# Block 0's rows of heads 2 to 7 by casting DMA issues ahead of the constants, and one ring of three PSUM tiles for its turns and scores

## The chip, the cores and the metric

One NeuronCore of one Trainium2 chip runs the kernel. The metric is the device time of one execution in microseconds. Before the change it is 240.57 us, the median of 7 runs (240.35 to 241.47).

## The reference, cut to what matters

Chunked attention with a small memory goes straight into a gated feed-forward layer:

```python
q, k, v: (4, 8, 768, 64)    mem_k, mem_v: (4, 8, 8, 64)      # batch, heads, tokens, width
for each chunk of 32 tokens:
    k_full = [mem_k, k[start-16 : start+32+8]]               # 8 memory rows, then the neighbourhood
    a = softmax(q_chunk @ k_full.T / 8);  out_chunk = a @ v_full
x = out as (3072 tokens, 512)
y = (relu(x @ w_gate) * (x @ w_val)) @ w_out                 # 512 -> 1536 -> 512, float32 out
```

## The kernel before, in words

The 3072 tokens are worked in 8 blocks of 384 (`TB`); two blocks make one batch entry. A block is cut into 4 pieces of 96 queries (`NQ`, `QB`), and the key window of each piece has 128 rows: 8 of memory and 120 of the sequence. Heads go in 4 pairs, called `hp`. All matmuls are in 16 bits.

Three kinds of work make a block. **Attention** turns keys and queries so that the head width lies on partitions, multiplies them to scores, takes the exponential on ScalarE, sums it and multiplies it with the values. **The first layer** is 12 units (`ffn_unit`, 4 gate and 4 value matmuls of 128x384 each, then a Relu on ScalarE at L340 and a product on VectorE at L341). **The second layer** is 3 output units (`out_unit`, 12 matmuls of 128x512 and a copy). While TensorE runs the layers of block n, the attention of block n+1 is woven between the units.

The order on every engine is written by hand (`tc.manual_schedule()`, L69): each engine does its instructions in the order of the source, and waits where data or a buffer is missing. The change touches the first three blocks:

- **Start.** `kst` and `qst` (L80, L81) hold float32 rows of block 0's keys and queries for heads 0 to 3. They come in two parts each by the hardware queues of SyncE and ScalarE (L384 to L388) and are cast by `cast` (L445) on VectorE and ScalarE. Heads 4 to 7 come by issues of GpSimd that cast on the way (`load_rows`, L125, L436, L438). GpSimd first makes the constants `ident` and `sel` (L431 to L434), then fetches the whole `mem_v` into `memv` (L435), then these rows, then block 0's value windows (`load_band`, L130, called at L439), `memk`, and the first weights (`load_w`, 256 columns of both matrices at a time, L442 and L443). SyncE copies the memory rows of `memv` into the value windows by `load_mem_v` (L149).
- **Block 0's attention** (L461 to L509). `fill` (L379) keeps TensorE running until the rows are there. `turn_pe` (L177) turns keys and queries of one pair by matmuls against `sel` and `ident` into a PSUM tile, `turn_copy` (L196) brings it to SBUF. `step_s0` (L236) makes mask and scores, and the exponential `ex` (L245). `wide_d` (L272) sums `ex` by matmuls into `xs` and takes the logarithm in place (L278); `wide_e` (L280) makes the reciprocal `rw` of it by an exponential (L282). `wide_v` (L285) multiplies with the values into `xo` and scales into `xT` (L291). The PSUM tiles of the kernel fill 8 banks of 128x512 float32: `xo` and `xs` take one each, the tile `sc` of the pool `sps` two, and the other four are first two turn tiles (`tps`), later the four banks of the units (`fps`).
- **Unit chunks.** The first two units are opened together, and each `chunk(0, f)` (L456) needs only pair f of `xT`, so that they start as soon as the first pair is done.
- **Block 1** (L524 to L558). Its turns, scores (`step_s`, L248), sums and products stand between units 2 to 11 of block 0.
- **Block 2** (L614, L615, in `run`, L585). While the units of block 1 run, `run` places pair hp's turn after the unit `at[hp] - 1`, its scores after the unit `at[hp]`, and its products inside the unit `at[hp] + 2`. From block 3 on, keys and queries are turned by DMA.

Of the kernel before, what the change touches and what calls it, by code (L numbers as in the profile page):

```python
# [17 lines left out]
def kernel(  # L18
# [12 lines left out]
    nc = tc.nc  # L31
# [33 lines left out]

    sps = ctx.enter_context(tc.tile_pool(name="sps", bufs=1, space=bass.MemoryType.PSUM))
    xps = ctx.enter_context(tc.tile_pool(name="xps", bufs=1, space=bass.MemoryType.PSUM))
# [11 lines left out]
    sels = [const.tile([128, NQ, 32], F16, name=f"sel{p}") for p in range(2)]  # L79
    kst = const.tile([KR + 2, H // 2, J * D], F32, name="kst")  # L80
    qst = const.tile([QR, H // 2, J * D], F32, name="qst")  # L81
    k16s = [const.tile([128, NQ, H, D], F16, name=f"k16{p}") for p in range(2)]

    vwins = [const.tile([128, NQ, H, 2 * D], F16, name=f"vwin{p}") for p in range(2)]
    qbds = [const.tile([128, NQ, HP, 2, QB], F16, name=f"qbd{p}") for p in range(2)]
    memk, memv = (const.tile([NMEM, B * H, D], F16, name=nm) for nm in ("memk", "memv"))
    ones = const.tile([128, 3, D], F16, name="ones")
    bias = const.tile([128, 3], F32, name="bias")
# [31 lines left out]
    def load_rows_mem(dma, dst, n, h0, nh):  # L120
        src = bass.AP(tensor=mem_k.tensor, offset=mem_k[n // 2, h0, 0, 0].offset,
                      ap=[[J * D, 2], [NMEM * D, nh], [1, J * D]])
        dma(dst, src)

    def load_rows(n, h0, nh):  # L125
        rk, rq = rows_of(n)
        pool_dma(rk[0:KR, h0:h0 + nh], k_rows(n, h0, nh))
        pool_dma(rq[:, h0:h0 + nh], q_rows(n, h0, nh))

# [47 lines left out]
    def turn_pe(n, hp):  # L177

        if n != 1:
            pool, tag = (pools["t"], "t") if n == 0 else (sps, "sc")  # L180
            ps = pool.tile([128, 2, 512], F32, tag=tag, name="kq_ps")
            kps, qps = ps[:, 0], ps[:, 1, 0:TB]
        else:
            ps, kps, qps = None, bank("k_ps"), bank("q_ps")[:, 0:TB]
        turns[n, hp] = ps, kps, qps
        rk, rq = (t.rearrange("p h (j d) -> p h j d", j=J) for t in rows_of(n))
        sel = sels[n % 2].rearrange("p i t -> p (i t)")

        for t, dst, w in ((rk, kps, sel[0:KR + 2]), (rq, qps, ident[:QR, :QR])):
            steps = dst.rearrange("p (r j) -> p j r", j=J) if n == 0 else dst.rearrange("p (j r) -> p j r", j=J)  # L190
            for j in range(J):
                for hh in range(2):
                    nc.tensor.matmul(steps[D * hh:D * hh + D, j], lhsT=t[:, 2 * hp + hh, j], rhs=w,
                                     start=True, stop=True)

    def turn_copy(n, hp):  # L196
# [5 lines left out]
        ps, kps, qps = turns.pop((n, hp))  # L202
        if n == 0:
            dve_copy(turns[n][:, hp], ps.rearrange("p a c -> p (a c)")[:, 0:512 + TB])
# [31 lines left out]
    def step_s0(n, hp):  # L236

        sc = sps.tile([128, 2, 512], F32, tag="sc", name="sc_ps")
        mq = bass.AP(tensor=maskq.tensor, offset=maskq.offset, ap=[maskq.ap[0], [0, NQ], [1, QB]])
# [8 lines left out]
    def step_s(n, hp):  # L248
        sc = sps.tile([128, 2, 512], F32, tag="sc", name="sc_ps")
        view = sc[:, :, 0:TB].rearrange("p a (c m) -> p a c m", m=QB)  # L250
# [21 lines left out]
    def wide_d(n, hp):  # L272
        ex = exs[n, hp]
        for i0, i1, kind in ((0, 1, 1), (1, NQ, 0)) if n == 0 else ((0, NQ - 1, 0), (NQ - 1, NQ, 2)):
            for hh in range(2):
                nc.tensor.matmul(xs[D * hh:D * hh + D, QB * i0:QB * i1], lhsT=ones[:, kind, :],
                                 rhs=ex[:, hh, i0:i1, :], start=True, stop=True)
        nc.scalar.activation(xs, xs, ACT.Ln, scale=1.0 / 64.0)  # L278

    def wide_e(n, hp):  # L280
        rinv = rpool.tile([128, TB], F32, tag="rw", bufs=4, name="rw")
        nc.scalar.activation(rinv, xs, ACT.Exp, scale=-1.0, bias=mln64)  # L282
        rinvs[n, hp] = rinv

    def wide_v(n, hp):  # L285
        ex = exs.pop((n, hp))
        for i in range(NQ):
            for hh in range(2):
                nc.tensor.matmul(xo[D * hh:D * hh + D, QB * i:QB * i + QB], lhsT=vwins[n][:, i, 2 * hp + hh, 0:D],  # L289
                                 rhs=ex[:, hh, i, :], start=True, stop=True)  # L290
        nc.vector.tensor_tensor(out=x_of(n)[:, hp, :], in0=xo, in1=rinvs.pop((n, hp)), op=ALU.mult)  # L291

# [27 lines left out]
    def ffn_open(n, ms, spare=False):  # L320
# [3 lines left out]
        for m in ms:  # L324
            if spare:
                sc = sps.tile([128, 2, 512], F32, tag="sc", name="gv_ps")
                pair = sc[:, 0, 0:TB], sc[:, 1, 0:TB]
# [55 lines left out]

    for hp in range(HP // 2):  # L384
        sp(kst[0:KR, 2 * hp:2 * hp + 2], k_rows(0, 2 * hp, 2))
        act_dma(qst[:, 2 * hp:2 * hp + 2], q_rows(0, 2 * hp, 2))
        if hp == 0:
            load_rows_mem(sp, kst[KR:KR + 2], 0, 0, H // 2)  # L388
    nc.scalar.preload_act_table_set("natural_log_exp_and_others")

    def words(t):
        return t.bitcast(U32)

    zero(words(filler), 0)


# [33 lines left out]

    nc.gpsimd.memset(words(ident), 0)  # L431
    nc.gpsimd.memset(words(sels[0].rearrange("p i t -> p (i t)")), 0)
    select(ident, 1.0, 0, [[-1, 128]], 1)
    build_sel(0)  # L434
    fetch_mem(memv, mem_v)  # L435
    load_rows(0, 4, 2)  # L436
    load_rows_mem(pool_dma, rows_of(0)[0][KR:KR + 2, H // 2:H], 0, H // 2, H // 2)
    load_rows(0, 6, 2)  # L438
    load_band(0, v, vwins)  # L439
    load_mem_v(0)  # L440
    fetch_mem(memk, mem_k)
    load_w(0, 256)  # L442
    load_w(256, 512)  # L443

    def cast(t, hp, eng):  # L445
        dst, src, n = rows_of(0)[t], (kst, qst)[t], (KR + 2, QR)[t]
        eng(dst[0:n, 2 * hp:2 * hp + 2], src[:, 2 * hp:2 * hp + 2])

# [11 lines left out]

    with tc.tile_pool(name="tps", bufs=2, space=bass.MemoryType.PSUM) as pools["t"]:  # L461
        fill(12)
        cast(0, 0, dve_copy)
        for t, hp in ((1, 0), (1, 1), (0, 1)):
            cast(t, hp, act_copy)
        turn_pe(0, 0)
        turn_copy(0, 0)
        fill(4)
        step_s0(0, 0)
        turn_pe(0, 1)  # L470
        turn_copy(0, 1)
        wide_d(0, 0)
        wide_e(0, 0)
        step_s0(0, 1)
        turn_pe(0, 2)
        turn_copy(0, 2)
        wide_d(0, 1)
        wide_e(0, 1)
        turn_pe(0, 3)
        turn_copy(0, 3)  # L480
    pools["f"] = ctx.enter_context(tc.tile_pool(name="fps", bufs=4, space=bass.MemoryType.PSUM))
    step_s0(0, 2)
    wide_v(0, 0)
    wide_d(0, 2)
    step_s0(0, 3)
    wide_e(0, 2)


    build_sel(1)
    load_rows_mem(pool_dma, rows_of(1)[0][KR:KR + 2], 1, 0, H)  # L490
    load_rows(1, 0, 4)
    load_rows(1, 4, 4)

    select(bias, NEG, -NMEM, [[-32, 3]], 1, ALU.is_ge)
    select(bias, 0.0, -NMEM, [[0, 3]], 1, ALU.is_ge)
    select(bias, NEG, NMEM + 55, [[32, 3]], -1, ALU.is_ge)
    load_w(512, 768)
    load_w(768, 1024)

    ffn_open(0, (0, 1))  # L500
    wide_v(0, 1)
    wide_d(0, 3)
    wide_e(0, 3)
    chunk(0, 0)
    wide_v(0, 2)
    chunk(0, 1)
# [3 lines left out]
    ffn_close(0)  # L510
    zero(vwins[1][96:128, NQ - 1, :, 0:D], 0.0)
    load_band(1, v, vwins)
    load_mem_v(1)
    load_w(1024, 1280)
    load_w(1280, 1536)
    load_rows_mem(pool_dma, rows_of(2)[0][KR:KR + 2], 2, 0, H)
    load_rows(2, 0, 4)
    load_rows(2, 4, 4)

    def sums(n, hp):  # L520
        wide_d(n, hp)
        wide_e(n, hp)

    ffn_unit(0, 2, spare=True)  # L524
    ffn_unit(0, 3)
    turn_pe(1, 0)
    turn_copy(1, 0)
    turn_pe(1, 1)
    turn_copy(1, 1)
    step_s(1, 0)  # L530
    turn_pe(1, 2)
    turn_copy(1, 2)
    ffn_unit(0, 4)
    step_s(1, 1)
    sums(1, 0)
    ffn_unit(0, 5)
    turn_pe(1, 3)
    turn_copy(1, 3)
    step_s(1, 2)
    sums(1, 1)  # L540
    ffn_unit(0, 6)
    step_s(1, 3)
    ffn_unit(0, 7)
    wide_v(1, 0)
    sums(1, 2)
    ffn_unit(0, 8)
    wide_v(1, 1)
    sums(1, 3)
    one_words(0, 0, 128, 0, 1, ONE)
    ffn_unit(0, 9)  # L550
    wide_v(1, 2)
    one_words(0, 0, NMEM + 16, 0, 1, 0)
    one_words(0, 0, NMEM, 0, 1, ONE)
    ffn_unit(0, 10)
    wide_v(1, 3)
    one_words(0, 0, 128, 1, 2, ONE)
# [5 lines left out]
    for a in range(0, NDC, 4):  # L562
        pool_dma(wo[:, a:a + 4, :], wo_src[:, a:a + 4, :])
    zero(words(k16s[0][0:32, 0].rearrange("p h d -> p (h d)")), 0)
    zero(words(k16s[1][96:128, NQ - 1].rearrange("p h d -> p (h d)")), 0)

# [18 lines left out]
    def run(order, n, at, turn_at):  # L585
        for u, (b, x) in enumerate(order):
# [3 lines left out]
            inner, outer = ("ve", "") if x >= NDC else ("v", "e")  # L590
            unit(b, x, [lambda w=(w, hp): pieces(n, [w]) for hp in now for w in inner])
            pieces(n, [(w, hp) for hp in now for w in outer])
            if n < NB:
                pieces(n, [("s", hp) for hp in range(HP) if u == at[hp]])
            if n == 2:
                for hp in range(HP):
                    if u == at[hp] - 1:
                        turn_pe(n, hp)
                        turn_copy(n, hp)
                if u < len(clear):  # L600
                    clear[u]()
            if u == turn_at and n + 1 < NB:
# [46 lines left out]
```

## Time and profile before

| What | Value |
|---|---|
| median of 7 runs | 240.57 us |
| the profiled execution, its own time | 241.84 us |
| its span, first to last instruction | 239.9 us |
| mean granted TensorE clock | 0.986 |
| TensorE / ScalarE / GpSimd / VectorE busy | 229.6 / 142.3 / 101.5 / 105.5 us |
| DMA, mean over the span | 115 GB/s, 107831 packets |
| unit 2 of block 0 starts on TensorE | 23.48 us |
| first turn of block 1 | 26.17 us |
| unit 0 of block 1 | 43.60 us |
| first output unit | 66.53 us |

The profile is one execution taken by the hardware profiler, on its one core. A line of the time order gives start and length in microseconds, the engine, the source line, the operation, what it writes and reads, how many, and in brackets the idle time before it with what ended that. Matmuls overlap, so their lengths are longer than the distance of their starts. In a table of stretches each engine has its busy time and its instruction count, then come the granted TensorE clock (1.00 is full), the busy share of the DMA engines and GB/s. In the table of waits a line names the engine and line that waited, for whom, and the total, the number and the longest.

### The profile page before, as it was taken

To read this page: it belongs to the slowest core of one execution; us is meant where nothing else is said; L and a number is where in the kernel's file an instruction comes from. 1 tells how busy PE (TensorE), PEld (TensorE's weight loads), DVE (VectorE), ACT (ScalarE), POOL (GpSimd) and SP (SyncE) were. 2 spreads that over 40 slices of the span, in tenths; PEclk is the share of its full clock that TensorE was granted. 3 is DMA by queue.
4 is the path that set the end of the run, shared out by engine and by line. 5 is a ranking of instruction groups with operands and counts; after the bars stand their busy time and mean duration, and the time that the engine had idled before them with its cause. 6 is when DMAs were issued, how large, how long until landed. Compare 5 with 4: busy or idle time off the path is not lost.

```text
span 239.9 us, 4610 instructions
## 1 busy us (share of the span) xinstructions
PE 229.6 (96%) x1736; PEld 132.4 (55%) x1736; DVE 105.5 (44%) x208; ACT 142.3 (59%) x300; POOL 101.5 (42%) x129
## 2 busy tenths in 40 slices
PE   7969899999899999999999999999999999999993
PEld 4634555655544566646664566546664666556641
DVE  3442846878621046521663055604642166313400
ACT  3671497277644288926984579728892698434321
POOL 8997766857039800794069501990220000000000
PEclk9985999999999999999999999999999999999999
DMA  7999999999987999299929998699901100120012
GB/s 163 135 163 193 194 179 194 179 198 151 149 117 91 198 128 154 44 146 170 155 54 98 162 190 75 42 190 152 137 3 60 71 3 0 43 91 0 1 44 87
DMA packets 107831, 27.61 MB, mean 115 GB/s; under 512 B 91730, under 2 KB 104866, under 8 KB 107810
## 3 DMA queue, kind: packets, MB, share of 16 engines
q0 software_dynamic: 82560, 15.16, 78.8%
q1 hardware_dynamic: 21378, 5.61, 20.4%
q10 hardware_dynamic: 3872, 6.56, 8.3%
q8 instruction: 13, 0.21, 0.4%
q14 instruction: 8, 0.07, 0.1%
HBM read 31.13 MB, written 6.29 MB: 156 GB/s over the span
## 4 chain that ended last, share of the span: by engine, by line
PE 81%; DVE 5%; POOL 4%; DMA 4%; ACT 3%; issue 2%; POOLq 0%; DVEq 0%
PE o_ps L360 25%; PE g_ps L334 24%; PE v_ps L334 23%; DMA wv<-in_moe_w_val_dram 3%; PE sc_ps L258 3%; DVE kq L207 3%; DVE gv L341 2%; PE xo_ps L298 2%; PE xs_ps L298 2%; POOL vwin L136 2%; PE sc_ps L233 1%; PE xo_ps L289 1%; ACT gr L340 1%; DMA out_dram<-o_sb 1%; ACT ln L302 1%
## 5 line engine op out<-in xcount | busy, mean ns | idle before, releaser
L341 DVE TENSOR_TENSOR gv<-v_ps,gr 128x384 f16<-128x384 f32 x95 | 52.8, 557 | 98.0 <-ACT gr L340 86.7
L334 PE MATMUL v_ps<-xT,wv 128*128 128x384 f16 x380 | 79.5, 329 | 0.4 <-DMA wv<-in_moe_w_val_dram 0.4
L334 PE MATMUL g_ps<-xT,wg 128*128 128x384 f16 x380 | 79.7, 330 | 0.0
L360 PE MATMUL o_ps<-wo,gv 128*128 128x512 f16 x288 | 63.5, 379 | 0.0
L340 ACT ACTIVATE gr<-g_ps 128x384 f16<-128x384 f32 x95 | 46.1, 487 | 21.9 <-PE g_ps L334 11.9
L334 PEld LDWEIGHTS <-wv 128*128 128x128 f16 x384 | 36.6, 99 | 22.9 <-DMA wv<-in_moe_w_val_dram 0.8
L334 PEld LDWEIGHTS <-wg 128*128 128x128 f16 x384 | 36.3, 98 | 23.0 <-issue 1.0
L360 PEld LDWEIGHTS <-gv 128*128 128x128 f16 x288 | 28.1, 98 | 32.9
L221 POOL COPY qbd<-qT 64x1536 f16<-64x1536 f16 x10 | 14.6, 1462 | 59.6 <-DMA qT<-q16n 59.3
L264 ACT ACTIVATE ex<-sc_ps,bias 128x256 f16<-128x256 f32 x84 | 33.4, 468 | 7.2 <-PE sc_ps L233 6.5
L369 ACT COPY o_sb<-o_ps 128x512 f32<-128x512 f32 x23 | 13.5, 586 | 39.2 <-PE o_ps L360 33.2
L136 POOL DMA_DIRECT2D vwin<-in_v_dram x32 | 29.0, 924 | 3.4 <-PE v_ps L334 1.0
L307 ACT ACTIVATE rinv<-ln,mln 64x768 f32<-64x768 f32 x24 | 22.1, 923 | 0.0
L302 ACT ACTIVATE ln<-xo_ps 64x384 f32<-64x384 f32 x24 | 11.7, 487 | 14.7 <-PE xs_ps L298 14.7
L136 POOL DMA_DIRECT2D k<-in_k_dram x20 | 17.8, 900 | 0.6 <-issue 0.6
L313 DVE TENSOR_TENSOR xT<-xo_ps,rinv 64x384 f16<-64x384 f32 x24 | 13.1, 547 | 10.2 <-ACT rinv L307 10.2
L162 POOL DMA_DIRECT2D q16n<-in_q_dram x20 | 15.5, 796 | 4.2 <-DMA wo<-in_moe_w_out_dram 4.2
L313 DVE TENSOR_TENSOR xT<-xs_ps,rinv 64x384 f16<-64x384 f32 x24 | 13.2, 551 | 0.7
L298 PEld LDWEIGHTS <-vwin 128*128 128x128 f16 x192 | 10.8, 98 | 3.2
L302 ACT ACTIVATE ln<-xs_ps 64x384 f32<-64x384 f32 x24 | 11.4, 474 | 0.0
L298 PE MATMUL xo_ps<-ex,vwin 128*128 128x96 f16 x96 | 11.1, 206 | 0.0
L298 PE MATMUL xs_ps<-ex,vwin 128*128 128x96 f16 x96 | 11.1, 206 | 0.0
(73 smaller groups left out, 134.1 us busy)
## 6 DMA issues: line engine op xcount, KB each, us to landing
out_dram<-o_sb ACTq DMA_DIRECT2D x23, 256.0 KB
vwin<-in_v_dram POOLq DMA_DIRECT2D x24, 120.0 KB, 8.6
q16n<-in_q_dram POOLq DMA_DIRECT2D x20, 96.0 KB, 5.6
k<-in_k_dram POOLq DMA_DIRECT2D x15, 120.0 KB, 4.4
wg<-in_moe_w_gate_dram POOLq DMA_DIRECT2D x6, 256.0 KB, 7.8
wv<-in_moe_w_val_dram POOLq DMA_DIRECT2D x6, 256.0 KB, 8.1
wo<-in_moe_w_out_dram POOLq DMA_DIRECT2D x3, 512.0 KB, 9.9
rk<-in_k_dram POOLq DMA_DIRECT2D x4, 224.0 KB, 8.6
```

The costliest lines, as they stand in the source:

```text
L136: pool_dma(dsts[p][NMEM + m0:NMEM + m1, i, :, 0:D], src)
L162: pool_dma(q16s[n][:, i], src)
L221: nc.gpsimd.tensor_copy(qbds[n % 2][s, :, :, hh, :].rearrange("p i a m -> p (i a) m"), qTs[n][s].rearrange("p i a m -> p (i a) m"))
L264: nc.scalar.activation(flat[:, :, :, s], view[:, :, :, s], ACT.Exp, scale=SCALE, bias=bias[:, g:g + 1])
L298: nc.tensor.matmul((xo, xs)[hh][:, QB * i:QB * i + QB], lhsT=vw[:, i, 2 * hp + hh, :], rhs=ex[:, hh, i, :], start=True, stop=True)
L302: nc.scalar.activation(ln[:, hh], (xo, xs)[hh][D:128], ACT.Ln, scale=1.0 / 64.0)
L307: nc.scalar.activation(rinv, lns.pop((n, hp)), ACT.Exp, scale=-1.0, bias=mln64[0:D, :])
L313: nc.vector.tensor_tensor(out=x_of(n)[D * hh:D * hh + D, hp, :], in0=(xo, xs)[hh][0:D], in1=rinv[:, hh, :], op=ALU.mult)
L334: nc.tensor.matmul(ps[a], lhsT=(wg, wv)[a][:, f, 128 * m:128 * m + 128], rhs=xTs[n][:, f, :], start=(f == 0), stop=(f == NFC - 1))
L340: nc.scalar.activation(gr, g_ps, ACT.Relu)
L341: nc.vector.tensor_tensor(out=gvs[n][:, m, :], in0=v_ps, in1=gr, op=ALU.mult)
L360: nc.tensor.matmul(o_ps, lhsT=gvs[n][:, m, 128 * t:128 * t + 128], rhs=wo[:, m, :], start=(m == 0), stop=(m == NDC - 1))
```

## The change

Only heads 0 and 1 of block 0 come by the hardware queues, as one issue for keys and one for queries; SyncE also brings the memory values of batch entry 0 as float32 (`mem32`), cast to `mem16` on VectorE. VectorE copies `mem16` into the 4 value windows of block 0, GpSimd into those of block 1, so that `memv` and `memk` are fetched later. GpSimd issues the rows of heads 2 and 3 and the keys of heads 4 to 7 before it makes `ident` and `sel`, whose clearing goes to VectorE, and the queries of heads 4 to 7 after them. In block 0 the turns and scores take turns in one ring of three tiles of two banks each; their order changes, `sps` opens only after that ring is closed, 10 fills stand in place of 12 and 4. The logarithm of `wide_d` goes to `rw` instead of staying in `xs`, and `wide_e` is joined to it. In block 1 all four turns and two scores stand before unit 4, the products of all four pairs stand between units 9 and 10, and they alternate between `xo` and `xs`. In block 2 the turn of a pair stands inside the unit `at[hp] - 1`, between its gate and value matmuls. The third weight part is issued ahead of the selects for `bias`, block 1's values after the fifth.

```diff
-    kst = const.tile([KR + 2, H // 2, J * D], F32, name="kst")
-    qst = const.tile([QR, H // 2, J * D], F32, name="qst")
+    kst = const.tile([KR + 2, 2, J * D], F32, name="kst")
+    qst = const.tile([QR, 2, J * D], F32, name="qst")
...
-            pool, tag = (pools["t"], "t") if n == 0 else (sps, "sc")
+            pool, tag = (pools["t"], "t") if n == 0 else (pools["s"], "sc")
...
-        if n == 0:
+        if n == 0 and hp == 0:
+            dve_copy(turns[n][:, hp, 0:512], kps)
+            act_copy(turns[n][:, hp, 512:], qps)
+        elif n == 0:
             dve_copy(turns[n][:, hp], ps.rearrange("p a c -> p (a c)")[:, 0:512 + TB])
...
     def step_s0(n, hp):
-        sc = sps.tile([128, 2, 512], F32, tag="sc", name="sc_ps")
+        sc = pools["t"].tile([128, 2, 512], F32, tag="t", name="sc_ps")
...
-        nc.scalar.activation(xs, xs, ACT.Ln, scale=1.0 / 64.0)
-
-    def wide_e(n, hp):
         rinv = rpool.tile([128, TB], F32, tag="rw", bufs=4, name="rw")
-        nc.scalar.activation(rinv, xs, ACT.Exp, scale=-1.0, bias=mln64)
+        nc.scalar.activation(rinv, xs, ACT.Ln, scale=1.0 / 64.0)
+        nc.scalar.activation(rinv, rinv, ACT.Exp, scale=-1.0, bias=mln64)
...
     def wide_v(n, hp):
+        xo_ = xs if n == 1 and hp % 2 else xo
...
-    for hp in range(HP // 2):
-        sp(kst[0:KR, 2 * hp:2 * hp + 2], k_rows(0, 2 * hp, 2))
-        act_dma(qst[:, 2 * hp:2 * hp + 2], q_rows(0, 2 * hp, 2))
-        if hp == 0:
-            load_rows_mem(sp, kst[KR:KR + 2], 0, 0, H // 2)
+    sp(kst[0:KR], k_rows(0, 0, 2))
+    act_dma(qst, q_rows(0, 0, 2))
+    load_rows_mem(sp, kst[KR:KR + 2], 0, 0, 2)
+    sp(mem32, bass.AP(tensor=mem_v.tensor, offset=mem_v[0, 0, 0, 0].offset,
+                      ap=[[D, NMEM], [NMEM * D, H], [1, D]]))
...
-    nc.gpsimd.memset(words(ident), 0)
-    nc.gpsimd.memset(words(sels[0].rearrange("p i t -> p (i t)")), 0)
+    load_k(0, 2, 2)
+    load_rows_mem(pool_dma, rows_of(0)[0][KR:KR + 2, 2:H], 0, 2, H - 2)
+    load_q(0, 2, 2)
+    load_k(0, 4, 4)
     select(ident, 1.0, 0, [[-1, 128]], 1)
     build_sel(0)
-    fetch_mem(memv, mem_v)
-    load_rows(0, 4, 2)
-    load_rows_mem(pool_dma, rows_of(0)[0][KR:KR + 2, H // 2:H], 0, H // 2, H // 2)
-    load_rows(0, 6, 2)
+    load_q(0, 4, 4)
     load_band(0, v, vwins)
-    load_mem_v(0)
-    fetch_mem(memk, mem_k)
     load_w(0, 256)
     load_w(256, 512)
...
+    with tc.tile_pool(name="tps", bufs=3, space=bass.MemoryType.PSUM) as pools["t"]:
+        fill(10)
+        dve_copy(rows_of(0)[0][0:KR + 2, 0:2], kst)
+        act_copy(rows_of(0)[1][:, 0:2], qst)
+        dve_copy(mem16, mem32)
+        mem_values = [lambda i=i: dve_copy(vwins[0][0:NMEM, i, :, 0:D], mem16) for i in range(NQ)]
+        mem_values[0]()
         turn_pe(0, 0)
         turn_copy(0, 0)
-        fill(4)
-        step_s0(0, 0)
         turn_pe(0, 1)
         turn_copy(0, 1)
-        wide_d(0, 0)
-        wide_e(0, 0)
-        step_s0(0, 1)
+        step_s0(0, 0)
+        for i in range(1, NQ):
+            mem_values[i]()
         turn_pe(0, 2)
         turn_copy(0, 2)
-        wide_d(0, 1)
-        wide_e(0, 1)
+        step_s0(0, 1)
+        wide_d(0, 0)
         turn_pe(0, 3)
         turn_copy(0, 3)
+        step_s0(0, 2)
+        wide_d(0, 1)
+        step_s0(0, 3)
     pools["f"] = ctx.enter_context(tc.tile_pool(name="fps", bufs=4, space=bass.MemoryType.PSUM))
-    step_s0(0, 2)
+    pools["s"] = ctx.enter_context(tc.tile_pool(name="sps", bufs=1, space=bass.MemoryType.PSUM))
     wide_v(0, 0)
     wide_d(0, 2)
-    step_s0(0, 3)
-    wide_e(0, 2)
+    wide_v(0, 1)
...
     ffn_open(0, (0, 1))
-    wide_v(0, 1)
+    wide_v(0, 2)
     wide_d(0, 3)
-    wide_e(0, 3)
     chunk(0, 0)
-    wide_v(0, 2)
     chunk(0, 1)
     wide_v(0, 3)
...
-    turn_pe(1, 0)
-    turn_copy(1, 0)
-    turn_pe(1, 1)
-    turn_copy(1, 1)
+    for hp in range(2):
+        turn_pe(1, hp)
+        turn_copy(1, hp)
     step_s(1, 0)
-    turn_pe(1, 2)
-    turn_copy(1, 2)
+    for hp in range(2, HP):
+        turn_pe(1, hp)
+        turn_copy(1, hp)
+    step_s(1, 1)
+    wide_d(1, 0)
     ffn_unit(0, 4)
-    step_s(1, 1)
-    sums(1, 0)
+    step_s(1, 2)
+    wide_d(1, 1)
     ffn_unit(0, 5)
-    turn_pe(1, 3)
-    turn_copy(1, 3)
-    step_s(1, 2)
-    sums(1, 1)
+    step_s(1, 3)
+    wide_d(1, 2)
     ffn_unit(0, 6)
-    step_s(1, 3)
+    wide_d(1, 3)
     ffn_unit(0, 7)
-    wide_v(1, 0)
-    sums(1, 2)
+    one_words(0, 0, 128, 0, 1, ONE)
     ffn_unit(0, 8)
-    wide_v(1, 1)
-    sums(1, 3)
-    one_words(0, 0, 128, 0, 1, ONE)
     ffn_unit(0, 9)
-    wide_v(1, 2)
+    for hp in range(HP):
+        wide_v(1, hp)
...
-            unit(b, x, [lambda w=(w, hp): pieces(n, [w]) for hp in now for w in inner])
+            turning = [hp for hp in range(HP) if n == 2 and u == at[hp] - 1]
+            unit(b, x, [lambda hp=hp: (turn_pe(n, hp), turn_copy(n, hp)) for hp in turning]
+                 + [lambda w=(w, hp): pieces(n, [w]) for hp in now for w in inner])
```

## The prediction

> **What bounds the kernel now.** I read the page's slices first (TensorE full after about 24 us), then the table of stretches, the order of time around 12 to 24 us, the chain that ended last, and the waits. From the 66.53 us mark TensorE never stops, so a microsecond won before it is kept. The page:
>
> ```profile
> PE 229.6 (96%) x1736; PEld 132.4 (55%) x1736; DVE 105.5 (44%) x208; ACT 142.3 (59%) x300; POOL 101.5 (42%) x129
> PEclk9985999999999999999999999999999999999999
> ```
>
> The clock line has one hole, at 12 to 24 us. The table of stretches places it:
>
> ```profile
> 12.00:13.00 1.00, 1.00 (x20) 0.54 (x17) 0.95 (x2) 0.83 (x2) 1.00 (x2) 1.00 1.73 125
> 15.00:16.00 1.00, 0.47 (x16) 0.30 (x11) 0.41 (x1) 0.77 (x2) 1.00 (x3) 1.00 1.41 180
> 16.00:17.00 1.00, 0.44 (x4) 0.18 (x3) 0.14 (x1) 0.51 (x2) 0.62 (x2) 0.61 1.47 191
> 17.00:18.00 1.00, 0.56 (x4) 0.14 (x3) 0.00 (x0) 0.84 (x2) 0.93 (x3) 0.50 1.52 199
> 22.00:23.00 1.00, 1.00 (x5) 0.49 (x4) 0.10 (x1) 0.00 (x0) 1.00 (x2) 0.50 1.44 194
> 23.00:24.00 1.00, 1.00 (x8) 0.60 (x7) 0.30 (x1) 0.83 (x2) 1.00 (x2) 0.98 1.45 196
> ```
>
> TensorE (first column) is half idle from 15 us, the clock halves inside the slice at 16 (0.61 = 22% full, so at 16.22) and is back at 23.04. Two idle stretches stand around it in the order of time:
>
> ```profile
> 16.56 0.53 PE L276 MATMUL xs_ps<-ex,ones 128*64 128x96 f16 x4 [1.08 <-ACT rw L282]
> 17.96 0.50 PE L334 MATMUL v_ps<-xT,wv 128*128 128x384 f16 x1 [0.44 <-DMA wv<-in_moe_w_val_dram]
> ```
>
> The first is `xs` waiting for the exponential that still reads it. The second is the first value weights. The chain says why they are late: GpSimd's issue queue from the start, then one long flight:
>
> ```profile
> 1.85 0.83 POOL memv L139
> ...
> 9.55 0.67 POOL memk L139
> ...
> 10.95 6.97 DMA wv<-in_moe_w_val_dram
> ```
>
> The waits hold the third thing, the scores of blocks 1 and 2 behind the copies of their turns:
>
> ```profile
> PE sc_ps L233 <- DVE kq L207: 2.9, 6, 0.7
> ```
>
> Four of the six are block 2's, 0.50 or 0.51 each in the order of time.
>
> **The queue and the start.** GpSimd loses `memv` (0.85 us) and `memk` (0.72) ahead of the weights, two clears (0.15 each), and keeps as many row issues (0.6 to 0.76 each; those of four heads took 0.72 to 0.76). Its first issue starts at 0.81 instead of 1.83, its value weights at 0.81 + 0.70 + 0.60 + 0.65 + 0.73 + 0.76 (selects, 0.29 + 0.47) + 0.67 + 3.7 (values) + 0.84 = 9.5 instead of 10.95. The flight shortens too: SyncE's small copies out of `memv` go until later, and by the packet records the 512-byte packets ran at 240 to 340 per us at 13 to 16 us beside these copies, and at 380 after them. Values (3,700 packets of 128 bytes at about 950 per us) start when the rows are done, about 7.3, and land by about 11.8 (before 13.3); gate and value weights follow at 1.33 us each, 13.2 and 14.5 (before 16.6 and 17.92). Needed below: 13.4 and 16.1. Three us of slack cover an error here.
>
> First, heads 0 and 1 by hardware. The first key part landed at 4.67, with the second queued behind it, so its loss speeds nothing: cast at 4.7, turn at 5.2 as before. Rows on the casting queue took 3.6 to 4.8 us from issue to landing: heads 2 and 3 land at about 5.8, after 448-packet issues the last keys at 7.3, the last queries (issued 4.25) at 8.4. Their turns come at 6.5 and 8.35: no stall, or 0.5 if the first packets wait until 4.87 as in this trace. `ident` and `sel` are ready at 4.25, 0.9 us ahead.
>
> In the program as built, the ScalarE half of pair 0's copy waits for VectorE's half: 0.68 + 0.5 us in a row for one copy of 1.09. The turn of pair 1 (1.0 us) covers it. The copies of `mem16` stand in no row; between a small clear (0.09) and the 114x512 cast (0.43), I take 0.25, near the cast. They stand on VectorE ahead of pair 2's copy and delay it by 0.75 (0.3 to 1.3), under scores of pair 1; beyond 1.5 TensorE would wait. GpSimd's four copies cost below 0.5 each (a third of the 64x1536 copy's 1.46), and delay only weights needed 10 us later.
>
> TensorE's list then adds up from its rows (turn 1.0, the first 1.3; mask and scores 0.85; sum and product 0.35 each): turn 0 until 6.5, turn 1 7.5, scores 0 8.35, turn 2 9.3, scores 1 10.15, sum 0 10.5, turn 3 11.45, scores 2 12.3, sum 1 12.65, scores 3 13.4, product 0 13.75. On ScalarE ex takes 0.81, Ln 0.47, Exp 0.58: ex 3 until 14.9, Ln 2 15.3, Exp 2 15.9, Exp 3 17.1. `xs` is now free after the Ln, so the 1.08 wait goes. Late next is `xo`: product, 0.12, scaling 0.55, again. Products 1 and 2 start at 14.5 and 15.5, sum 3 ends at 16.1, and chunk 0 runs from there. Chunks 1 and 2, product 3 and its scaling (until 18.5) and chunk 3 give unit 2 at **19.2 at full clock, against 23.48**: −4.3.
>
> **The clock.** Between 12.81 and 16.22 TensorE idles 1.15 us by this list. The slices of before give 2.2 busy us in those 3.4, mine 2.3: nearly the same. [...] But before, the longest gap was 1.08 us, and it dropped. I take the row: it drops at 16.2 again. [...] The sixteen matmuls, 0.16 each at full clock, cost 0.32 until 19.63; unit 2 at 20.8: **−2.7**.
>
> [...]
>
> **Block 1.** Scores are drawn ahead and turn 3 stands before unit 4, so ScalarE's work is packed into units 4 to 7. Starts of ScalarE in the order of time:
>
> ```profile
> 32.71 0.48 ACT L340 ACTIVATE gr<-g_ps 128x384 f16<-128x384 f32 x1
> 33.09 1.21 ACT L264 ACTIVATE ex<-sc_ps,bias 128x256 f16<-128x256 f32 x3
> 34.18 0.50 ACT L278 ACTIVATE xs_ps<-xs_ps 128x384 f32<-128x384 f32 x1
> 34.71 0.58 ACT L282 ACTIVATE rw<-xs_ps,mln 128x384 f32<-128x384 f32 x1
> 35.19 0.48 ACT L340 ACTIVATE gr<-g_ps 128x384 f16<-128x384 f32 x1
> ```
>
> One round takes 35.19 − 32.71 = 2.48 us; TensorE's round (unit 1.30 to 1.40, scores 0.27, sum 0.28) takes 1.95. Three rounds must wait 0.53 each. Walked through from the first turn: scores 1 wait 0.4 for ex 0 and the single `sc`, scores 3 wait 0.25, sum 2 0.1, sum 3 0.8; products 2 and 3, now back to back, wait 0.68 and 0.15 for the scaling. Less the 0.3 or so of waits that go, block 1's first turn to unit 0 of block 1 takes 19.5 instead of 17.43: **+2.05**. Were ScalarE's lengths to add without overlap (0.48 + 1.20 + 0.50 + 0.58 = 2.76), it would be +2.95.
>
> **Block 2.** The turn stands 0.65 us earlier and its copies (1.15) are queued ahead of the unit's product, not behind it. The scores come 0.5 + 0.65 + 1.30 = 2.3 us after the turn, so the four waits go: **−2.05**. The product on VectorE is late by 1.1, with 4 banks in hand.
>
> Later loads move up with the stream (values of block 1, `memv`, `memk`: landed by 36, used from 38).
>
> **Sum.** −2.7 + 2.05 − 2.05 = −2.7. On the profiled execution: 241.84 − 2.7 = 239.1, of which 1.9 lie outside the span. That one is 1.27 above the median; the forecast is 240.57 − 2.7 = **237.9**.
>
> **Rivals.**
> [...]
> - *The casting queue is late* (the move doesn't give heads 2 to 7 earlier): first packets at 4.87 at the soonest, turns 1 and 2 wait, and ten fills end at 4.7, half a us before the turn, so that the clock may rise late. Some 1.5 us: 239.4.
> - *A drop in block 1 too*, one window: 1.7 us, 239.6. The idle 0.25, 0.1 and 0.8 lie within 3.2 us; that is 70% busy, close to what dropped before.
> - *Slower: ScalarE piles up in block 1.* Place: units 4 to 7. If its instructions don't overlap (+2.95) TensorE idles 3 us there, the clock halves for two windows as before (6.8 us at half, 3.4 lost): −2.7 + 0.9 + 3.4 = +1.6, 242.2. It decides once the granted clock is 0.5 through units 6 to 9. Against it: the starts above do overlap.
>
> **The numbers.** Likeliest 0.42; no drop 0.13; late queue 0.15; one drop in block 1 0.15; pile-up 0.15. The range takes in all but the last and some of the edges: 236.2 to 241.0. Faster by over 0.3% (0.72 us, about what a measurement can tell) holds the first two and most of the next two, 0.73; within it 0.12; slower 0.15.
>
> **What would show it.** Unit 2 at 20.8, clock 0.5 from about 16.2 to 19.6 only, value weights landed before 16, no wait of sums for Exp; idle before sums and products in block 1 of about 2.4 in all; no wait of scores for copies in block 2. Wrong if turns 1 or 2 wait for rows, if the clock is low elsewhere, or if block 1 takes over 20.5.

## The result and the profile after

The changed kernel takes **238.43 us** (median of 12 runs, 237.99 to 240.13) against 240.57 of 31 runs before on the same chip: ratio 0.9921, 95% interval 0.9904 to 0.9938 (taken over the runs, not from the two medians). The forecast was 237.9. The profiled execution is the slowest of the twelve: 240.13, where 239.1 was forecast for it, with a span of 238.2 us (before 239.9). The page's lines for the engines and the clock:

```profile
PE 226.6 (95%) x1730; PEld 131.7 (55%) x1730; DVE 107.4 (45%) x215; ACT 141.1 (59%) x299; POOL 103.9 (44%) x131
PEclk9997999999999999999999999999999999999998
```

One hole is left in the clock line, and it is shorter. The table of stretches places it:

```profile
18.00:19.00 1.00, 1.00 (x5) 0.33 (x3) 0.00 (x0) 0.00 (x0) 0.47 (x1) 0.63 1.44 189
19.00:20.00 1.00, 1.00 (x11) 0.61 (x11) 0.25 (x1) 0.00 (x0) 0.93 (x2) 0.50 1.46 196
20.00:21.00 1.00, 1.00 (x5) 0.47 (x4) 0.31 (x1) 0.00 (x0) 0.78 (x4) 0.50 1.46 197
21.00:22.00 1.00, 1.00 (x6) 0.50 (x4) 0.09 (x1) 0.55 (x2) 1.00 (x2) 0.66 1.44 194
```

0.63 and 0.66 put the half clock between 18.26 and 21.68: 3.41 us, and not at the 16.22 of before. A stretch of 3.41 us at half clock is called a window from here on; the profile before had two. It shows in a run's mean clock as well, as half of 3.41 is 0.7% of 240: runs with a window have 0.993 or less, runs without 0.996 or more.

TensorE's waits in the start, in the order of time:

```profile
5.20 0.63 PE L199 MATMUL kq_ps<-sel,rk 114*64 114x128 f16 x8 [0.55 <-POOL sel L429]
...
8.09 0.63 PE L199 MATMUL kq_ps<-sel,rk 114*64 114x128 f16 x8 [0.29 <-DMA rk<-in_k_dram]
9.48 0.52 PE L199 MATMUL kq_ps<-ident,rq 96*64 96x96 f16 x8 [0.77 <-DMA rq<-in_q_dram]
...
14.48 0.36 PE L297 MATMUL xo_ps<-ex,vwin 128*64 128x96 f16 x8 [0.37 <-DVE xT L299]
15.55 0.36 PE L297 MATMUL xo_ps<-ex,vwin 128*64 128x96 f16 x8 [0.72 <-DVE xT L299]
16.25 0.34 PE L342 MATMUL g_ps<-xT,wg 128*128 128x384 f16 x1 [0.17 <-DMA wg<-in_moe_w_gate_dram]
17.48 0.34 PE L342 MATMUL v_ps<-xT,wv 128*128 128x384 f16 x1 [0.90 <-DMA wv<-in_moe_w_val_dram]
```

The wait of `xs` for the exponential is gone, and products 1 and 2 wait for the scaling at 14.48 and 15.55, as forecast (14.5 and 15.5). But the rows of turn 2 and the first weights are waited for. The chain that ended last says when these weights were issued, and how long they flew:

```profile
9.50 0.23 POOL wg L172
...
10.27 7.16 DMA wv<-in_moe_w_val_dram
```

The value weights were issued at 10.27, 0.7 us sooner than before, and landed at 17.43 instead of 17.92. Last, the table of stretches for block 1 (first turn to unit 0 of block 1) and block 2 (from there to the first output unit); the first number after the comma is TensorE's busy time:

```profile
24.59:44.08 19.49, 16.78 (x209) 10.52 (x209) 11.65 (x24) 12.01 (x28) 16.15 (x21) 1.00 1.71 177
44.08:64.72 20.64, 20.64 (x219) 12.34 (x216) 17.53 (x32) 13.25 (x31) 11.10 (x14) 1.00 1.75 156
```

The same two before:

```profile
26.17:43.60 17.43, 16.58 (x209) 9.77 (x209) 11.64 (x24) 11.98 (x28) 11.82 (x16) 1.00 1.71 185
43.60:66.53 22.93, 20.90 (x218) 12.34 (x215) 18.27 (x35) 13.92 (x31) 10.98 (x13) 1.00 1.94 171
```

TensorE's idle time grew from 0.85 to 2.71 in block 1 and fell from 2.03 to nothing in block 2. Its waits in block 1 after:

```profile
26.44 0.35 PE L242 MATMUL sc_ps<-kq 64*128 64x96 f16 x8 [0.70 <-DVE kq L216]
28.15 0.35 PE L242 MATMUL sc_ps<-kq 64*128 64x96 f16 x8 [0.28 <-ACT ex L273]
35.17 0.36 PE L285 MATMUL xs_ps<-ex,ones 128*64 128x288 f16 x4 [0.74 <-ACT rw L288]
40.71 0.36 PE L297 MATMUL xo_ps<-ex,vwin 128*64 128x96 f16 x8 [0.72 <-DVE xT L299]
```

So the profiled pair gives: start −1.58 (unit 2 at 21.90 instead of 23.48), block 1 +2.06, block 2 −2.29, the rest within 0.1; sum −1.8.

### The profile page after: what moved, and what is told of

Same layout as the page of the kernel before. It is cut to its first block, busy times and chain, and to the rows that moved or that the text cites. A ratio compares the mean times of both kernels' runs of the same rounds, so it can differ in the third digit from the quotient of the medians.

```text
span 238.2 us, 4591 instructions
## 1 busy us (share of the span) xinstructions
PE 226.6 (95%) x1730; PEld 131.7 (55%) x1730; DVE 107.4 (45%) x215; ACT 141.1 (59%) x299; POOL 103.9 (44%) x131
## 4 chain that ended last, share of the span: by engine, by line
PE 85%; DMA 4%; POOL 3%; ACT 3%; issue 2%; DVE 1%; POOLq 0%; DVEq 0%; ACTq 0%
PE g_ps L342 26%; PE v_ps L342 26%; PE o_ps L368 25%; DMA wv<-in_moe_w_val_dram 3%; PE sc_ps L267 3%; PE xo_ps L306 2%; ACT ex L273 2%; PE xs_ps L306 2%; POOL vwin L142 2%; PE kq_ps L199 1%; DMA out_dram<-o_sb 1%; PE sc_ps L242 1%; POOL rk L127 1%; PE gv_ps L342 1%; ACT rw L288 0%
## 5 line engine op out<-in xcount | busy, mean ns | idle before, releaser
L342 PEld LDWEIGHTS <-wg 128*128 128x128 f16 x384 | 36.8, 98 | 23.4 <-issue 0.5
L321 DVE TENSOR_TENSOR xT<-xs_ps,rinv 64x384 f16<-64x384 f32 x24 | 13.2, 551 | 0.7
```

Source lines behind the costliest of these rows:

```text
L321: nc.vector.tensor_tensor(out=x_of(n)[D * hh:D * hh + D, hp, :], in0=(xo, xs)[hh][0:D], in1=rinv[:, hh, :], op=ALU.mult)
L342: nc.tensor.matmul(ps[a], lhsT=(wg, wv)[a][:, f, 128 * m:128 * m + 128], rhs=xTs[n][:, f, :], start=(f == 0), stop=(f == NFC - 1))
```

## The experiments

The stretches below are cut at the same two instructions in each kernel. Ratios are to the kernel before on the same chip; its medians on the three chips are 240.46 (e7, e9, e9c, e10), 240.62 (e1 to e4) and 240.76 (e5b, e11, e12).

**e7, block 2's turns alone.** The kernel before, with the turn put between the halves of the unit:

```diff
-            unit(b, x, [lambda w=(w, hp): pieces(n, [w]) for hp in now for w in inner])
+            turning = [hp for hp in range(HP) if n == 2 and u == at[hp] - 1]
+            unit(b, x, [lambda hp=hp: (turn_pe(n, hp), turn_copy(n, hp)) for hp in turning]
+                 + [lambda w=(w, hp): pieces(n, [w]) for hp in now for w in inner])
...
-            if n == 2:
-                for hp in range(HP):
-                    if u == at[hp] - 1:
-                        turn_pe(n, hp)
-                        turn_copy(n, hp)
```

> The kernel before with one part of the change alone: block 2's turns placed inside the unit, ahead of its second half. Theory (the place of the turns is worth about 2 us whatever the start is): the stage from unit 0 of block 1 to the first output unit falls from 22.93 to about 20.8, time 240.6 - 2.0 = 238.6. Rival (the waits of the scores only hid another limit, a load or VectorE's backlog, so that the gain needs the earlier start or the new load order): stage 22 or more, time 240 to 240.6.

238.43 us, ratio 0.9928 (0.9907 to 0.9949): the whole gain of the change. Four of its 11 runs had a window; the seven without have a median of 238.1, the changed kernel's ten 238.3. The stretches of this kernel, and a wait in the first of them:

```profile
23.28:41.70 18.42, 16.93 (x210) 9.60 (x209) 11.64 (x24) 11.97 (x28) 12.86 (x18) 1.00 1.64 189
41.70:62.48 20.78, 20.75 (x217) 12.34 (x216) 17.87 (x34) 13.23 (x31) 11.58 (x14) 1.00 1.94 171
27.35 0.82 PE L334 MATMUL v_ps<-xT,wv 128*128 128x384 f16 x4 [0.60 <-DMA wv<-in_moe_w_val_dram]
```

Block 2 runs without a gap (20.75 busy of 20.78), so the theory holds. The first line tells something else. Up to 41.70 the program is that of before, yet its stretch starts at 23.28 and not at 26.17: this execution had no window. And block 1 then takes 18.42, not 17.43, with a wait of 0.60 for value weights that the profile before did not have. So both marks of the profile before, 26.17 and 17.43, were those of an execution with two windows, and in this pair 1 us of the late start came back in block 1.

**e1, block 2's turns undone** in the changed kernel (the same edit backwards).

> The changed kernel with block 2's turns put back behind the scores, outside the unit. Theory (the stage of block 1's units lost 2.29 us because the copies of a turn no longer stand behind the unit's product on VectorE): the four waits of 0.5 us come back, that stage takes about 22.9 us instead of 20.64, the rest stays; time 238.4 + 2.2 = 240.6. Rival (the stage got shorter because the load and start work of block 2 moved, not because of the turns' place): the stage stays at 20.6 to 21, time 238.4 to 238.8.

240.21 us, ratio 0.9979 (0.9964 to 0.9994), 1.8 above the changed kernel.

```profile
22.79:42.27 19.48, 16.78 (x209) 10.52 (x209) 11.66 (x24) 11.99 (x28) 15.21 (x21) 1.00 1.66 184
42.27:64.75 22.48, 20.91 (x218) 12.35 (x216) 17.73 (x33) 13.91 (x31) 12.95 (x16) 1.00 1.80 163
```

1.57 us idle in block 2, in three waits of 0.51, the first of them

```profile
52.82 0.34 PE L242 MATMUL sc_ps<-kq 64*128 64x96 f16 x8 [0.51 <-DVE kq L216]
```

One of the four was not there: the first turn's copies started on VectorE 3.53 us after the stretch began, against 3.99 before. None of the 12 runs had a window. Both ways the turns' place is worth 1.8 to 2.2.

**e2, block 1's order of before** in the changed kernel:

```diff
-        xo_ = xs if n == 1 and hp % 2 else xo
+        xo_ = xo
...
-    for hp in range(2, HP):
-        turn_pe(1, hp)
-        turn_copy(1, hp)
+    turn_pe(1, 2)
+    turn_copy(1, 2)
+    ffn_unit(0, 4)
     step_s(1, 1)
     wide_d(1, 0)
-    ffn_unit(0, 4)
+    ffn_unit(0, 5)
+    turn_pe(1, 3)
+    turn_copy(1, 3)
...
```

> The changed kernel with block 1's order of before (scores one by one, turn 3 after unit 5, sums and products between units 7 and 11, products all in one PSUM tile). Theory (ScalarE is packed into units 4 to 7 and the products wait for each other: that is the 2.06 us by which the stage from block 1's first turn to unit 0 of block 1 grew): the stage falls from 19.49 to about 17.4 and nothing is given back later; time 238.4 - 2.05 = 236.4. Rival (the later half of the stage's gain is only an advance that the next stage gives back, as block 2's scores or weights are then late): stage 17.4, the next 22 or more, time 238 to 238.4.

238.34 us, ratio 0.9910 (0.9891 to 0.9930): nothing won. The stretch took 19.71, and its waits in the order of time are others:

```profile
24.59 0.35 PE L242 MATMUL sc_ps<-kq 64*128 64x96 f16 x8 [0.70 <-DVE kq L216]
26.43 0.82 PE L342 MATMUL v_ps<-xT,wv 128*128 128x384 f16 x4 [0.23 <-DMA wv<-in_moe_w_val_dram]
31.89 0.34 PE L242 MATMUL sc_ps<-kq 64*128 64x96 f16 x8 [0.18 <-DVE kq L216]
35.18 0.60 PE L297 MATMUL xo_ps<-ex,vwin 128*64 128x96 f16 x4 [1.33 <-DMA vwin<-in_v_dram]
```

ScalarE's wait is gone, and the old order asks for block 1's values 1.33 us before they land: the change issues them behind the weights of units 8 and 9. The theory had the waits that go, but not the load that takes their place in the same stretch; the rival had the time, but sought the loss in the next stretch, which took 20.63.

**e9 and e9c, the values ahead of those weights**, with the order of e2 (e9) and with the order of the change (e9c):

```diff
+    load_band(1, v, vwins)
     load_w(1024, 1280)
...
-    load_band(1, v, vwins)
     load_w(1280, 1536)
```

> The changed kernel with block 1's order of before and, besides, block 1's values issued ahead of the weights for units 8 and 9 (as the kernel before had it). With the order alone TensorE still idled 2.44 us in that stage, 1.33 of it for block 1's values. Theory (two limits of the same size lie one behind the other: ScalarE and the products in the order of the change, the load of block 1's values in the order of before): the values land about 2.7 us earlier, the wait of 1.33 goes, 0.3 comes back for the weights of unit 8; stage about 18.4, time 238.3 - 1.2 = 237.1. Rival (the queue is full, so whatever is issued first delays the other by as much, and unit 8 waits over 1 us for its weights): stage 19.2 or more, time 238.0 to 238.4.

> The changed kernel with block 1's values issued ahead of the weights for units 8 and 9, nothing else. Theory (with the order of the change the values are needed only after unit 9, so their landing limits nothing, and unit 8's weights still land in time): same time, 238.4, same idle of TensorE in block 1 (2.0 to 2.4 us). Rival (the load order itself was worth something in the changed kernel): 237.8 or less, or over 239 if unit 8 waits for weights.

e9 took **237.21 us** (four runs), ratio 0.9871 (0.985 to 0.9893), the stretch 18.88; e9c 238.22, ratio 0.9921 (0.9899 to 0.9943), the stretch 19.48 as in the change. So two limits stood one behind the other: undoing either alone gives nothing, undoing both 1.2. What is left in e9 is weights (order of time):

```profile
24.35 0.34 PE L242 MATMUL sc_ps<-kq 64*128 64x96 f16 x8 [0.70 <-DVE kq L216]
25.56 0.82 PE L342 MATMUL g_ps<-xT,wg 128*128 128x384 f16 x4 [0.35 <-DMA wg<-in_moe_w_gate_dram]
26.96 0.82 PE L342 MATMUL v_ps<-xT,wv 128*128 128x384 f16 x4 [0.58 <-DMA wv<-in_moe_w_val_dram]
```

e9 also shows what the new start can earn. It shares with e7 the order of blocks 1 and 2 and differs from it in the start, the order of later loads and the place of the logarithm. On the same chip it took 237.2 against the 238.1 of e7's runs without a window, and the spans of the two profiles are 235.5 and 235.9.

**e5b, the products apart again**, behind units 7 to 10 and in one PSUM tile, on top of e9c:

```diff
-        xo_ = xs if n == 1 and hp % 2 else xo
+        xo_ = xo
...
     ffn_unit(0, 7)
+    wide_v(1, 0)
+    ffn_unit(0, 8)
+    wide_v(1, 1)
...
-    for hp in range(HP):
-        wide_v(1, hp)
+    wide_v(1, 2)
...
+    wide_v(1, 3)
```

> The kernel of e9c (block 1's values issued ahead of the weights for units 8 and 9; 238.2) with one thing more: block 1's products stand behind units 7, 8, 9 and 10 again, all in one PSUM tile, instead of back to back behind unit 9. Scores and sums keep the order of the change. Theory (back to back they wait 0.72 and 0.2 for the scaling of the one before; apart they don't): those two waits go, the wait of 0.73 of sum 3 stays; stage 19.48 - 0.9 = 18.6, time 237.3. Rival (VectorE or the values' landing holds the first product behind unit 7 by as much): 238.0 to 238.4.

237.93 us, ratio 0.9886 (0.9849 to 0.9923); the stretch 19.09, 0.39 less instead of 0.9. The two waits of the products, 0.92 in all, are gone, but TensorE was busy for 17.15 us against 16.78 in e9c, which takes 0.37 back. Why it was busier isn't shown: this busy time differs by as much between the profile before (16.58) and e7 (16.93), whose programs are the same up to there. The wait of sum 3 for ScalarE stays:

```profile
33.31 0.36 PE L285 MATMUL xs_ps<-ex,ones 128*64 128x288 f16 x4 [0.74 <-ACT rw L288]
```

**e12, the same remedy for block 1's first turn**, inside unit 3, on top of e9:

```diff
-    ffn_unit(0, 3)
-    for hp in range(2):
-        turn_pe(1, hp)
-        turn_copy(1, hp)
+    ffn_unit(0, 3, [lambda: (turn_pe(1, 0), turn_copy(1, 0))])
+    turn_pe(1, 1)
+    turn_copy(1, 1)
```

> The kernel of e9 (block 1's order and value load of before; 237.2) with the remedy of block 2 used for block 1's first turn: it stands inside unit 3, ahead of that unit's second half, so that its copies are no longer queued behind the unit's product. Theory (the wait of 0.70 of the scores goes, but units 4 and 5 then wait for weights that land at 25 and 26.4 whatever TensorE does: 0.35 and 0.58 in e9 become about 1.5 together): time 237.0 to 237.3. Rival (the waits for weights in e9 are not limits of their own): 236.5.

237.47 us, ratio 0.9862 (0.9827 to 0.9898): not told from e9. The 0.70 is gone and stands in the weights' waits:

```profile
25.74 0.82 PE L342 MATMUL g_ps<-xT,wg 128*128 128x384 f16 x4 [0.76 <-DMA wg<-in_moe_w_gate_dram]
27.06 0.82 PE L342 MATMUL v_ps<-xT,wv 128*128 128x384 f16 x4 [0.50 <-DMA wv<-in_moe_w_val_dram]
...
35.76 0.82 PE L342 MATMUL v_ps<-xT,wv 128*128 128x384 f16 x4 [0.27 <-DMA wv<-in_moe_w_val_dram]
```

The two waits named in the expectation are 1.26 together, where about 1.5 was expected, and a third of 0.27 has come: 1.53 in all, against 1.63 in e9 with its 0.70. The matmuls that wait start at 25.74 and 27.06, against 25.56 and 26.96 in e9, though unit 2 started 0.5 later here (20.28 against 19.80). So the loads are the bound, and an earlier TensorE only waits longer.

**e3, TensorE kept busy in the start's gaps** by 12 matmuls of zeros:

```diff
     wide_d(0, 2)
+    keep(2)
     wide_v(0, 1)
...
     ffn_open(0, (0, 1))
+    keep(4)
     wide_v(0, 2)
     wide_d(0, 3)
+    keep(6)
     chunk(0, 0)
```

> The changed kernel with 12 extra matmuls of zeros (into a PSUM tile that nothing reads) in the gaps of TensorE at 14.1, 14.9 and 16.1 us: 0.3, 0.65 and 0.96 us of them. Theory (the clock fell to half for one window because of these gaps): no slice below 0.95 in 13 to 24 us, unit 2 starts 1.7 us earlier, at about 20.2, time 236.7. Rival (the clock falls at a fixed point, or for what lies before, whatever the gaps hold): the window at half stays, unit 2 at 21.9 or a little later, time 238.4 to 238.7.

239.94 us, ratio 0.9961 (0.9943 to 0.9979): 1.5 slower than the change. The remedy had a price that I had not seen: its PSUM tile was not free until an exponential of block 0 had ended.

```profile
14.98 0.48 PE L394 MATMUL keep_ps<-filler 128*128 128x384 f16 x2 [0.65 <-ACT ex L254]
```

Unit 2 started at 21.05, later than in any other profile of this start without a window (19.61 to 20.28). There was no window in the 12 runs (mean clock 0.998 to 1.0); but the changed kernel itself had one in 2 of 12 only, so this tells little of the cause.

**e4, the opening matmuls cut up**, to move TensorE's instruction fetch:

```diff
-        fill(10)
+        for i in range(80):
+            nc.tensor.matmul(xo[:, 0:48], lhsT=filler[:, 0:128], rhs=filler[:, 0:48], start=True, stop=True)
```

> The changed kernel with its ten opening matmuls of 384 columns cut into eighty of 48: the same columns, 70 instructions more. Theory (TensorE's fetch of 16 KB of instructions at 14.05 us sits on one DMA engine for 0.94 us, and this engine's part of every later load lands 1.3 us behind the others): the fetch comes some 70 instructions earlier, before 11 us, where the queue was still waiting for issues; the last part of the value weights then lands within 0.4 us of the others, at about 16.4 instead of 17.43, and unit 2 starts 0.9 us earlier; time 237.5. Rival (the part that lands last has nothing to do with the fetch): landings stay at 16.2 and 17.4, time 238.4.

238.43 us, ratio 0.9928 (0.9904 to 0.9953). In the trace, a load counts as landed when 16 parts have; in the changed kernel 15 parts of the gate weights had by 14.81 and the last at 16.20, 2.15 after the fetch of 16 KB began at 14.05. In e4 the fetch began at 6.72, and the last two parts of these weights came at 15.07 and 15.26, those of the value weights at 16.51 and 16.59. So the laggard went, and the time stayed: five of the 12 runs had a window, and the seven without have 238.2, the changed kernel's ten 238.3. But the fetch need not make a laggard: in e9 it began at 13.59, while the gate weights moved, and the last part was 0.01 behind for the gate weights and 0.43 for the value weights. What made the one in the changed kernel stays open; it isn't what sets the median.

**e10, twelve opening matmuls** instead of ten.

> The changed kernel with twelve opening matmuls of zeros instead of ten. In some profiles of kernels with this start the matmuls took twice as long until 9.7 us, in others only until about 5, and the gap ahead of the first turn was 0.55 to 0.86 us. Theory (the clock rises at the end of a busy window of about 3.4 us, and that gap spoils one window in some runs): without the gap the matmuls run at full speed by 6.5 us in every run, unit 2 at about 19.6 where no window at half follows; runs without such a window at 237.9 to 238.2, those with one at 239.4 to 240, and the latter are no fewer than before, so the median stays within 0.4 of 238.4. Rival (the gap doesn't matter): the same two kinds of start as with ten, same time.

238.31 us, ratio 0.9930 (0.9903 to 0.9956), no difference; two of the six runs had a window. What it was to repair is seen in the first turn of e1, whose program is that of the change up to block 2:

```profile
5.39 1.06 PE L199 MATMUL kq_ps<-sel,rk 114*64 114x128 f16 x8 [0.74 <-POOL sel L429]
```

In e1 matmuls took nearly twice as long until 10.3, not 9.7, as the expectation has it. The row of the table shows a clock of 1.00 there, but the trace's records of the clock begin only at 10.29, with full, and the row counts time without a record as full. In the changed kernel's profile and in e10's (0.63 for this turn) the records begin at 4.62 and 4.64, but then the rows were not there: 0.29 and 0.77, or 1.02 in e10. Either way unit 2 came at 19.8 to 20.3 wherever no window followed (e1, e2, e9, e9c, e10, e5b, e12; e4 19.61). So the slow clock early, which the rival of a late casting queue had named, was there in five of the eleven profiles with the new start (e1, e2, e5b, e9c, e12), and cost next to nothing. Whether twelve opening matmuls prevent it in every run isn't shown by the two profiles that have them (e10, e11).

**e11, rows by pairs of heads**, on top of e10:

```diff
-    load_k(0, 4, 4)
+    load_k(0, 4, 2)
...
-    load_q(0, 4, 4)
+    load_q(0, 4, 2)
+    load_k(0, 6, 2)
+    load_q(0, 6, 2)
     load_band(0, v, vwins)
```

> The kernel of e10 (twelve opening matmuls; 238.3) with the rows of heads 4 to 7 of block 0 in four issues instead of two, the keys and queries of heads 4 and 5 ahead of those of 6 and 7. Theory (the first value weights bound the start: they land at 16.6 to 17 whatever comes before, for the casting queue moves all bytes in order): turn 2's wait of 1.0 us for its queries shrinks to under 0.5, and what is won there is spent in the wait for the first value weights, which grows from 0.51 to about 1; two more issues on GpSimd change nothing or put the weights 0.3 later; unit 2 at 19.9 to 20.2, time 238.2 to 238.6. Rival (the rows bound the start): unit 2 at about 19.2, time 237.6.

240.54 us, ratio 0.9998 (0.9973 to 1.0022): 2.2 slower than e10, outside what theory and rival expected. The rows came in time, and two issues more on GpSimd put the values' landing from 13.30 to 14.61 and the first value weights from 16.89 to 17.83:

```profile
14.00 0.23 PE L297 MATMUL xo_ps<-ex,vwin 128*64 128x96 f16 x2 [1.04 <-DMA vwin<-in_v_dram]
14.66 0.23 PE L297 MATMUL xo_ps<-ex,vwin 128*64 128x96 f16 x2 [0.42 <-DMA vwin<-in_v_dram]
```

TensorE stood still from 13 to 14, and the clock fell for a window:

```profile
13.00:14.00 1.00, 0.00 (x1) 0.00 (x1) 0.00 (x0) 0.97 (x2) 1.00 (x3) 1.00 1.45 90
...
16.00:17.00 1.00, 0.31 (x9) 0.31 (x10) 0.81 (x2) 0.24 (x1) 1.00 (x2) 0.76 1.33 164
17.00:18.00 1.00, 1.00 (x12) 0.43 (x8) 0.58 (x2) 0.42 (x1) 0.91 (x2) 0.50 1.38 180
```

All 12 runs of e11 had a mean clock of 0.993 or less. A part of the 2.2 is this window: e10's two runs with one took 239.3 and 239.6. In this start GpSimd's issues ahead of the values have no slack.

## Why the prediction was right, and where it was not

The time fell as forecast and by nearly the forecast's size, but that the size fits is in part luck. Of the prediction's three signs of being wrong two came: turn 2 waited for its rows, and the clock was low elsewhere, from 18.26 instead of 16.2. Block 2 was right in its mechanism and its size. The gain of the start was put far too high and the cost of block 1 too high, and the two errors cancel in part.

- **Block 2, −2.05.** Right: −2.29 in the profiles; in e7 alone 2.0 of the time and 2.15 of the stretch; in e1 1.8 comes back. The wait of scores for copies is gone from block 2.
- **Block 1, +2.05.** The stretch took 19.49, 19.5 was forecast, with waits of 0.28, 0.74 and 0.72 where 0.4, 0.8 and 0.68 were expected; the smaller 0.25 and 0.1 did not come. But the comparison with 17.43 was too hard: with an early start the old order takes 18.42 (e7) and waits for weights. At like starts the new order costs 1.07. The rival of a pile-up in ScalarE didn't come: the granted clock stayed 1.00 through the stretch.
- **The start, −2.7.** This step failed in two places, the weights and the clock.
- **The weights.** "13.2 and 14.5 (before 16.6 and 17.92)" was forecast, and "Three us of slack cover an error here". They landed at 16.20 and 17.43 and were waited for, 0.17 and 0.90; these two make up the 1.1 by which unit 2, at 21.90, missed the forecast 20.8. GpSimd issued the value weights at 10.27, not 9.5: its first issue began at 1.36 instead of 0.81, for a reason that no run shows, and the values went out at 5.78, where its sum has 4.92. So the values landed 1.4 late, at 13.17 instead of 11.8. The weights moved at 324 to 341 packets of 512 bytes per us from 13 to 16 (238 to 340 before), not at 380, though SyncE's small copies were gone: some 0.25 more. The last 1.3 to 1.4 are a laggard, the last of the 16 parts (see e4). In e9 and e10, without one, the gate weights landed at 14.95 and 15.50, the value weights at 16.79 and 16.89. The slack was none, as e11 shows.
- **The clock.** "It drops at 16.2 again": I took the row of one execution for a property of the kernel. The window is not tied to the kernel's start: 16.22 before, 18.26 after, none in e1. No run shows a half clock from 16.2 that ends at 19.63, by which −4.3 became −2.7: it lasted from 16.22 to 23.04 before, from 18.26 to 21.68 in the changed kernel and from 16.52 to 19.94 in e11. The kernel before had a window in 42 of its 62 runs beside the experiments, the changed one in 2 of 12.
- **What the start is worth.** Between executions without a window, unit 2 moves from 20.58 (e7, whose start is that of before) to about 20.0: −0.6. With −0.6 + 1.07 − 2.29 the sum is −1.8. The ten runs of the change without a window have a median of 238.3; the 20 such runs of before beside the experiments have 240.1 to 240.3 by chip. This agrees. So start and block 1 together, forecast at −0.65, cost 0.5 by the profiles and 0.2 by e7's and the change's runs without a window. The further few tenths of the median are runs of before that had one.
- **Gaps and the clock.** A gap of over 1.1 us is not needed for a drop: before had a window in 42 of 62 runs with no gap over 1.1 us in its profile, e11 in all 12 with none over 1.04. Nor has the rise a fixed place: with the same start the records of full clock begin at 4.62 in one profile (the changed kernel) and at 10.29 in another (e1).
- **GpSimd beside VectorE's copies.** GpSimd's issues took 0.60 to 0.82 us for rows (0.60 to 0.71 before) and 3.72 for the four of values (3.68 before), beside six copies of 0.27 to 0.67 on VectorE. The two selects for `sel`, not issues, did take 0.65 instead of 0.47, 0.82 in e1; whether the copies beside them are the cause isn't shown.
- **Rows and small things.** Turn 1 didn't wait; turn 2 waited 1.06 for its rows (0 to 0.5 was forecast), as the queries of heads 4 to 7 went out at 5.09, not 4.25. `sel` was ready at 5.14, not 4.25, and the first turn waited for it last, yet began at 5.20 as forecast, since VectorE's cast of its keys ended only at 5.07. GpSimd's four copies of `mem16` took 0.60 each, not under 0.5.

So of the change as it stands, one moved line earns the time. The new start earns some tenths more where block 1 does not take them back. A version that keeps it and the new start, but has block 1's order and value load of before (e9), is faster than both kernels.

## What to carry to other kernels

Where a consumer waited for a copy queued behind another job of the copying engine, issuing its producer half a unit earlier won 2.0 us here (e7); look for this where the same short wait recurs. It won nothing where weights were waited for right behind it (e12, where waits of 1.53 took the place of 1.63). Before adding up stages of one profile, see whether its clock row shows a window that other executions needn't have: both the start and the stage after it, whose loads then have time to land, are read wrongly from it (23.28 and 18.42 in e7 without one, 26.17 and 17.43 before with two). Where removing a limit gives nothing, look for the next one at the same place and undo both (e2 and e9c gave 0.1 and 0.2, e9 1.2).

## What the runs showed of the hardware

- The records of the granted clock lie on a grid of 3.41 us, whose place differs from one execution to the next. Before, full clock begins at 5.98, half at 16.22 (three steps later), full at 23.04 (two more); in the changed kernel at 4.62, 18.27 (four steps) and 21.68; in e11 at 6.28, 16.52 and 19.94.
- In the step just ahead of these three drops TensorE was busy for 2.25, 1.65 and 0.99 us of 3.41. Over the 13 profiles, the end of the kernel included, every step at full clock with 1.08 or less was followed by half clock, none with 2.30 or more was, and in between both happened: no drop came behind 1.54 (before, from 234.67), 1.64 (e7, from 230.51) and 2.16 (e4, from 7.64). So in these profiles the busy time of the step went with the drops, but did not decide them alone; what else did stays open. Off the grid little busy time passes: e10 had only 1.82 from 13.60 to 17.01, and no drop.
- The rise to full clock came, in all 13, at the end of a step with TensorE busy for 2.97 or more. In the five profiles where it came late, at 9.0 to 10.3, the step before that one had 2.65 to 2.68 busy, with the gap ahead of the first turn in it. Before, a step at half clock with 2.63 (from 16.22) was not followed by a rise either.
- Two issues more on GpSimd's queue, of 0.64 and 0.67 us (e11), delayed the loads behind them by 0.9 to 1.3 us.
